# Attention and two MLPs on one core: the keys' products of a pair of heads as 24 matmuls of 64 rows and 128 columns in place of 12 of 128 rows and 256 columns

## The chip, the core and the metric

The kernel runs on one core of a Trainium2 chip. A core has TensorE (PE, with its weight loads PEld), VectorE (DVE), ScalarE (ACT), GpSimd (POOL), SyncE (SP) and 16 DMA engines. The metric is the device time of one execution in microseconds. The kernel before took 882.99 us, the median of three runs (882.97 to 883.67).

## The reference

Three stages follow each other: an attention with exponential features for 4 batches of 8 heads, and two MLPs over the 2304 rows that it gives.

```
def phi(x):                                   # x: 576 x 64 per head
    proj = x @ w_phi                          # w_phi: 64 x 128
    proj = proj - max(abs(proj), axis=-1)
    return concat([exp(proj), exp(-proj)])    # 576 x 256
q_p, k_p = phi(q), phi(k)
kv  = k_p.T @ v ;  z = sum(k_p, over the tokens)
out = (q_p @ kv) / (q_p @ z + 1e-06)
x = out.transpose(0, 2, 1, 3).reshape(2304, 512)
x = leaky(x @ w_in) @ w_out                   # leaky(h) = max(0.01 h, h), 512 -> 2048 -> 512
x = mish(x @ w_in2) @ w_out2                  # 512 -> 2048 -> 512
```

The change touches `k @ w_phi` and the subtraction of the largest absolute value behind it, for the first 512 of the 576 tokens.

## The kernel before

**Pairs and rounds.** The 32 heads are worked on as 16 pairs. `attention(n)` is one round, in which different pairs stand at different steps: pair n+2 is loaded and transposed, pair n+1 is multiplied by `w_phi` (`q_proj` for the queries, `k_proj` for the keys), pair n has its exponentials taken and its `kv` summed, pair n-1 is multiplied out (`nd`), and pair n-2 is normalised and turned back. Between them the weights of the first MLP are prepared (`extra`). The instructions of each engine run in the order in which this code writes them; PE, ACT and DVE each go through their own list and wait for each other by semaphores. Behind the attention come the two MLPs, some 740 of the 881 us.

**The keys' product.** A pair's keys lie transposed in `kth` and `ktl`, a high part rounded to fp32r and the remainder: 128 rows (two tokens of neighbouring places, 64 values each) by 512 columns (4 column groups of 128 for the two heads). `w_phi` lies in `wbh` and `wbl`, high and low part, as a block diagonal of 128 rows and 256 columns: the upper 64 rows meet the first 128 columns, the lower 64 rows the second, zeros elsewhere. One matmul takes a column group as its weights and streams the 256 columns of `wbh` or `wbl`; three such products (high by high, high by low, low by high) add up. A round has 12 of them: 6 into a PSUM tile `xt` (its pool has one buffer) and then 6 into a bank of the ring `a` (`bank("a")`, four banks in turn). The source line of all is L441.

**The guard.** `k_guard` takes each bank's maximum of the absolute values over 128 features (L429) and subtracts it (L430), on DVE. The result is `kd`, whose exponentials ACT takes a round later (L454).

**The queries' product** just ahead of it (`q_proj`, L469) is made of matmuls that use 64 rows of the array each, the upper and the lower half in turn, into four banks of the ring `a`; ACT copies these to `qd` (L471), and POOL takes the maximum over the partitions. The ring goes on: the keys' bank `a` is the one that held the first of the queries' four products.

**Behind the keys' block** stand on PE the products of the leftover tokens (L95 to L97, every other round), the transposes of the next pair (L402), the turning back (L561, into `xt` too), L535 and L512.

Of the kernel before, what the change touches and what calls it, by code (L numbers as in the profile page):

```python
# [9 lines left out]
F32 = mybir.dt.float32  # L10
# [10 lines left out]
def attention_two_mlps_kernel(  # L21
# [12 lines left out]
    nc = tc.nc  # L34
    B, H, S, D = q.shape
    NT, DM = out.shape
    DFF = w1_in.shape[1]
    F = w_phi.shape[1]
    P = 128
# [3 lines left out]
    NM = MAIN // P  # L43
# [26 lines left out]
    pa = tc.alloc_tile_pool(name="pa", bufs=1, space=PSUM)  # L70
    dr = tc.alloc_tile_pool(name="dr", bufs=1, space=bass.MemoryType.DRAM)
    ap = tc.alloc_tile_pool(name="ap", bufs=2, reuse_waits="tile")
# [3 lines left out]
    xt = {}  # L76
# [10 lines left out]
    def bank(ring):  # L87
        return rings[ring].tile([P, 512], F32, tag=ring, name=ring)
# [5 lines left out]
    def three(o, wh_, wl_, xh, xl, start=True, stop=True, **kw):  # L94
        nc.tensor.matmul(out=o, lhsT=wh_, rhs=xh, start=start, stop=False, **kw)  # L95
        nc.tensor.matmul(out=o, lhsT=wh_, rhs=xl, start=False, stop=False, **kw)  # L96
        nc.tensor.matmul(out=o, lhsT=wl_, rhs=xh, start=False, stop=stop, **kw)  # L97
# [40 lines left out]
    class Loads:  # L138
# [5 lines left out]
        def load(self):  # L144
            while not self.held and (self.rest or self.at < len(self.units) and places.open(places.stages)):
                self.half()
# [163 lines left out]
    with tc.manual_schedule():  # L310
# [28 lines left out]
        st = [dict() for _ in range(PAIRS)]  # L339
# [29 lines left out]
        def values(i):  # L369
            b, p = divmod(i, NP)  # L370
            h0 = 2 * p
            vm = st[i]["vm"] = vmain[i % NV]
            for h in range(2):
                nc.sync.dma_start(out=vm[:, h, :, 0:D], in_=v[b, h0 + h, 0:MAIN, :].rearrange("(p t) d -> p t d", t=NM))
            vl = st[i]["vl"] = vleft[i % NV]
            for r in range(2):
                nc.sync.dma_start(out=vl[r * LEFT:(r + 1) * LEFT, r, 0:D], in_=v[b, h0 + r, MAIN:S, :])
# [10 lines left out]
        wbh = ap.tile([P, 2 * F], F32R, name="wbh", bufs=1)  # L388
        wbl = ap.tile([P, 2 * F], F32R, name="wbl", bufs=1)
# [37 lines left out]
        def k_guard(src, n, kd):  # L427
            mx = ap.tile([P, n], F32, tag=f"mx{n}", name="mx")
            nc.vector.tensor_reduce(out=mx, in_=src, axis=AX.X, op=ALU.max, apply_absolute_value=True)  # L429
            nc.vector.tensor_tensor(  # L430
                out=kd, in0=src, in1=mx.unsqueeze(2).to_broadcast([P, n, F]), op=ALU.subtract)

        def k_proj(i, c, own=True):
            s = st[i]
            if c == 0:
                s["kd"] = ap.tile([P, 2, NM, F], F32, tag="kd", name="kd")
            t = pa.tile([P, 512], F32, tag="xt", name="xt") if c == 0 and own else bank("a")
            for n, (x, w) in enumerate((("kh", wbh), ("kh", wbl), ("kl", wbh))):
                for j in range(2):
                    u = slice((2 * c + j) * P, (2 * c + j + 1) * P)  # L440
                    nc.tensor.matmul(out=t[:, j * 2 * F:(j + 1) * 2 * F], lhsT=s[x][:, u], rhs=w,  # L441
                                     start=(n == 0 and j == 0), stop=(n == 2), skip_group_check=True)
            return lambda: k_guard(t.rearrange("p (n f) -> p n f", f=F), NM, s["kd"][:, c])

        def k_proj_left(i):
            l = lf[i // 2]
            l["kd"] = ap.tile([P, 2, F], F32, tag="kdl", name="kdl", bufs=1)
            t = bank("a")
            three(t[:, 0:2 * F], l["h"][:, 0:P], l["l"][:, 0:P], wbh, wbl)
            k_guard(t[:, 0:2 * F].rearrange("p (n f) -> p n f", f=F), 2, l["kd"])  # L450
# [6 lines left out]
        def q_proj(i, h):  # L457
            s = st[i]
            if "qd" not in s:
                s["qd"] = ap.tile([P, 2, S], F32, tag="qd", name="qd")  # L460
                s["qm"] = ap.tile([P, 2, S], F32, tag="qm", name="qm", bufs=1)
            todo = []
            for o in range(2):
                n = HM + (h == o) * LEFT
                todo.append((o, bank("a"), n, h * (HM + (1 - o) * LEFT), (1 - o) * (HM + h * LEFT)))
            for x, (w, q_) in enumerate(((wbh, "qh"), (wbh, "ql"), (wbl, "qh"))):
                for o, t, n, c0, d0 in todo:
                    r = slice(o * D, (o + 1) * D)
                    nc.tensor.matmul(out=t[:, 0:n], lhsT=w[r, o * F:(o + 1) * F], rhs=s[q_][r, c0:c0 + n], start=(x == 0), stop=(x == 2))  # L469
            for o, t, n, c0, d0 in todo:  # L470
                nc.scalar.activation(out=s["qd"][:, h, d0:d0 + n], in_=t[:, 0:n], func=AF.Copy)  # L471
            qd, qm = s["qd"][:, h, :], s["qm"][:, h, :]
            nc.gpsimd.partition_all_reduce(qm, qd, P, bass_isa.ReduceOp.absmax)  # L473
# [44 lines left out]
        def kv_copy(i):  # L518
            s = st[i]
            s["kv"] = ap.tile([P, 4, D + 1], F32, tag="kv", name="kv", bufs=1)  # L520
            nc.scalar.activation(out=s["kv"], in_=s["kvp"][:, 0:4 * (D + 1)].rearrange("p (c n) -> p c n", n=D + 1), func=AF.Copy)
# [48 lines left out]
        def left_exp(i, a):  # L570
            if i % 2 == 0:
                lf[i // 2].setdefault("lp", []).append(exp(lf[i // 2]["kd"], "lp", 1 - 2 * a))

        def q_exp_first(h):
            if "qp" not in st[0]:
                st[0]["qp"] = [ap.tile([P, 2, S], F32, tag=f"qp{sg}", name="qp", bufs=1) for sg in (1, -1)]
            for x in range(2):
                nc.scalar.activation(out=st[0]["qp"][x][:, h], in_=st[0]["qm"][h], func=AF.Exp, scale=float(1 - 2 * x))

        def q_exp(i):  # L580
            st[i]["qp"] = [exp(st[i]["qd"], "qp", sg) for sg in (1, -1)]

        def k_exp(i, a):
            st[i].setdefault("kp", []).append(exp(st[i]["kd"], "kp", 1 - 2 * a))
# [19 lines left out]
        def attention(n):  # L604

            x, o, w, p, t = (i if 0 <= i < PAIRS else None for i in range(n - 2, n + 3))
            x_copy = lambda: None
            if n + 3 < PAIRS:  # L610
                load(n + 3)
            loads.half()
            if t is not None and t > 1:
                values(t)
            loads.half()
            if n > 0:
                if p is not None:
                    q_proj(p, 0)
                    q_proj(p, 1)
                kv_copy(o)  # L620
            if n == 1:
                q_exp_first(1)
            if x is not None and n < PAIRS:
                normalise(x)
            if p is not None:
                k_proj(p, 0, t is not None)()
                k_proj(p, 1)()
                if p % 2 == 0:
                    k_proj_left(p)
            if w is not None:  # L630
                for a in range(2):
                    if n > 0:
                        left_exp(w, a)
                    k_exp(w, a)
                    if n == 0:
                        q_proj(p, a)
            if n == 0:
                for a in range(2):
                    left_exp(0, a)
            extra(n, 0)  # L640
            if n == PAIRS - 1:
                fill(0)
            if n == 0:
                transposes(t, "q", "l")
                q_left(t)
                q_guard_first(0)
                transposes(t, "k")
                q_guard_first(1)
                q_exp_first(0)
            elif t is not None:  # L650
                transposes(t)
                q_left(t)
            if x is not None:
                x_copy = x_t(x)
            x_copy()
            extra(n, 1)
            if o is not None:
                nd(o)
            if p is not None:
                q_guard(p)  # L660
            extra(n, 2)
            if w is not None:
                if n > 0:
                    q_exp(w)
                for a in range(2):
                    kv(w, a)
            if p is None:
                normalise(o)
            if n == PAIRS - 1:
                fill(1)  # L670
# [427 lines left out]
        while todo:  # L1098
            u = todo.pop(0)
# [45 lines left out]
        while todo:  # L1145
            u = todo.pop(0)
# [569 lines left out]
        for x in (10, 11):  # L1716
            t = place("s%d" % x, F32, 2, DM, pool=late[0], name="more")
# [27 lines left out]
        for x in range(2):  # L1745
            t = place("st%d" % x, F32, 2, DM, pool=gp, name="more")
# [15 lines left out]
        for s in range(2 * 4 * OPS):  # L1762
            sb, n, fp = steps3[s]
# [60 lines left out]
```

## Time and profile before

| what | value |
|---|---|
| median of three runs | 882.99 us |
| profiled execution | 883.12 us |
| its span, first to last instruction | 881.3 us |
| PE busy | 874.3 us (99%) |
| DVE busy | 633.3 us (72%) |
| ACT busy | 502.6 us (57%) |
| mean granted TensorE clock | 0.999 |

PE is busy nearly all the time. Busy time of PE overlaps in the records (a matmul is 280 to 390 ns long there, while the next starts 110 to 220 ns later), so the distance from one start to the next is what a matmul costs; durations only show when it was held up. The profile's page gives sums over the whole execution, and the attention is its first 141 us; the timelines below are from there.

### The profile page before, as it was taken

The numbers are of one execution on the slowest core, as the hardware profiler recorded it, in microseconds if no ns is written. First come the engines' busy times: TensorE is split into PE (matmuls) and PEld (weight loads), VectorE is DVE, ScalarE is ACT, GpSimd is POOL, SyncE is SP. The second block draws the span as 40 slices with busy tenths as digits, with TensorE's granted clock in tenths as the row PEclk, the third lists the DMA queues.
The fourth block names the chain that finished last, engine by engine and source line by source line (L and its number), as shares of the span: only waits on it lengthen the run. The fifth ranks groups of instructions, "written<-read, shape, count | busy, mean of one in ns | idle before, by whom it ended". The sixth has DMA issues, their size and how long they took to land.

```text
span 881.3 us, 17024 instructions
## 1 busy us (share of the span) xinstructions
PE 874.3 (99%) x6497; PEld 754.1 (86%) x6497; DVE 633.3 (72%) x1056; ACT 502.6 (57%) x828; POOL 78.5 (9%) x62
## 2 busy tenths in 40 slices
PE   9999999999999999999999999999999999999997
PEld 7999999888888888888988888888888888888887
DVE  8999998688988626889886328676655488655575
ACT  6899998656565545544454326444444477444442
POOL 4646452000000000000000000000000000000000
PEclk9999999999999999999999999999999999999999
DMA  6653430179788867899962454888875899876662
GB/s 176 173 144 99 110 103 3 61 251 324 265 291 275 287 229 251 253 375 362 348 202 85 136 177 171 292 313 274 304 258 188 283 371 397 235 226 221 201 179 60
DMA packets 145585, 197.28 MB, mean 224 GB/s; under 512 B 50912, under 2 KB 82272, under 8 KB 145504
## 3 DMA queue, kind: packets, MB, share of 16 engines
q1 hardware_dynamic: 116096, 143.36, 50.6%
q10 hardware_dynamic: 29408, 52.84, 17.1%
q8 instruction: 51, 0.84, 0.4%
q14 instruction: 30, 0.25, 0.1%
HBM read 119.60 MB, written 76.55 MB: 223 GB/s over the span
## 4 chain that ended last, share of the span: by engine, by line
PE 96%; ACT 2%; DMA 0%; DVE 0%; issue 0%; SPq 0%; ACTq 0%
PE b L95 14%; PE b L97 14%; PE b L96 14%; PE a L95 13%; PE a L96 13%; PE a L97 13%; PE outs L535 3%; PE kvp L512 3%; PE a L469 1%; PE a L402 1%; PE a L441 1%; PE xt L441 1%; PE xt L561 1%; PE kvp L515 1%; ACT qp L454 0%; ACT kp L454 0%
## 5 line engine op out<-in xcount | busy, mean ns | idle before, releaser
L92 DVE TENSOR_TENSOR g<-raw,g 128x1024 fp32r<-128x1024 f32 (+1 forms) x64 | 77.1, 1205 | 54.4 <-ACT g L91 54.3
L91 ACT ACTIVATE g<-raw 128x1024 fp32r<-128x1024 f32 (+1 forms) x64 | 66.9, 1046 | 66.5 <-PE b L97 37.0
L92 DVE TENSOR_TENSOR gl<-raw,gh 128x512 fp32r<-128x512 f32 x72 | 49.7, 690 | 60.0 <-ACT gh L91 57.7
L91 ACT ACTIVATE gh<-raw 128x512 fp32r<-128x512 f32 x72 | 45.2, 628 | 60.8 <-PE b L97 24.6
L473 POOL PARTITION_ALL_REDUCE qm<-qd x30 | 64.2, 2189 | 45.1 <-ACT qd L471 42.1
L96 PE MATMUL b<-gl,wo 128*128 128x512 f32 (+1 forms) x192 | 67.9, 354 | 0.0
L95 PE MATMUL b<-gh,wo 128*128 128x512 f32 (+1 forms) x192 | 67.9, 354 | 0.0
L97 PE MATMUL b<-gh,wo 128*128 128x512 f32 (+1 forms) x192 | 67.9, 354 | 0.0
L95 PE MATMUL b<-win,w 128*128 128x512 f32 x128 | 49.9, 390 | 0.0
L96 PE MATMUL b<-win,w 128*128 128x512 f32 x128 | 49.9, 390 | 0.0
L95 PE MATMUL a<-gh,wo 128*128 128x512 f32 x128 | 49.8, 389 | 0.0
L96 PE MATMUL a<-gl,wo 128*128 128x512 f32 x128 | 49.8, 389 | 0.0
L97 PE MATMUL a<-gh,wo 128*128 128x512 f32 x128 | 49.8, 389 | 0.0
L97 PE MATMUL b<-win,w 128*128 128x512 f32 x128 | 49.8, 389 | 0.0
L95 PE MATMUL b<-g,wo 128*128 128x512 f32 x128 | 49.8, 389 | 0.0
L96 PE MATMUL b<-g,wo 128*128 128x512 f32 x128 | 49.8, 389 | 0.0
L97 PE MATMUL b<-g,wo 128*128 128x512 f32 x128 | 49.8, 389 | 0.0
L917 DVE TENSOR_TENSOR g<-b,z 128x512 f32<-128x512 f32 x31 | 21.4, 689 | 36.2 <-PE b L97 33.4
L96 PEld LDWEIGHTS b<-gl,wo 128*128 128x128 f32 x192 | 36.3, 189 | 5.0
L97 PEld LDWEIGHTS b<-gh,wo 128*128 128x128 f32 x192 | 36.3, 189 | 5.0
L95 PEld LDWEIGHTS b<-gh,wo 128*128 128x128 f32 x192 | 36.3, 189 | 4.9
L1514 DVE TENSOR_TENSOR g<-g,g 128x512 f32<-128x512 f32 x32 | 22.1, 689 | 23.0 <-ACT g L1498 16.5
(325 smaller groups left out, 2535.5 us busy)
## 6 DMA issues: line engine op xcount, KB each, us to landing
raw<-gp SPq DMA_DIRECT2D x56, 512.0 KB, 5.4
raw<-gd ACTq DMA_DIRECT2D x72, 256.0 KB, 3.8
gd<-g ACTq DMA_DIRECT2D x70, 256.0 KB, 3.9
stage<-in_moe_w_out_dram SPq DMA_DIRECT2D x32, 512.0 KB, 5.6
gp<-g SPq DMA_DIRECT2D x64, 256.0 KB, 2.8
stage<-in_moe_w_in_dram SPq DMA_DIRECT2D x26, 512.0 KB, 6.0
gp<-g ACTq DMA_DIRECT2D x48, 256.0 KB, 3.1
scr<-more SPq DMA_DIRECT2D x24, 256.0 KB, 5.1
```

The source lines that it names most:

```text
L91: nc.scalar.activation(out=hi, in_=src, func=AF.Copy)
L92: nc.vector.tensor_tensor(out=lo, in0=src, in1=hi.bitcast(F32), op=ALU.subtract)
L95: nc.tensor.matmul(out=o, lhsT=wh_, rhs=xh, start=start, stop=False, **kw)
L96: nc.tensor.matmul(out=o, lhsT=wh_, rhs=xl, start=False, stop=False, **kw)
L97: nc.tensor.matmul(out=o, lhsT=wl_, rhs=xh, start=False, stop=stop, **kw)
L402: nc.tensor.transpose(out=t[:, j * P:(j + 1) * P], in_=s[nm + "n"].rearrange("p h t d -> p (h t d)")[:, j * P:(j + 1) * P], identity=ident)
L441: nc.tensor.matmul(out=t[:, j * 2 * F:(j + 1) * 2 * F], lhsT=s[x][:, u], rhs=w, start=(n == 0 and j == 0), stop=(n == 2), skip_group_check ...
L473: nc.gpsimd.partition_all_reduce(qm, qd, P, bass_isa.ReduceOp.absmax)
L512: nc.tensor.matmul(out=both[r, h, a, :], lhsT=s["kp"][a][:, h, t, r], rhs=s["vm"][:, h, t, :], start=(a == 0 and h == 0 and t == 0), stop= ...
L535: nc.tensor.matmul(out=g[u // 2][r, u % 2, h], lhsT=s["qp"][a][:, h, q0 + r.start:q0 + r.stop], rhs=s["kv"][:, 2 * h + a], start=(a == 0), ...
L917: nc.vector.tensor_tensor(out=c, in0=x["Y"], in1=cur[0].z7[n % 2], op=ALU.add)
L1514: nc.vector.tensor_tensor(out=out_, in0=in0, in1=in1, op=ALU.subtract)
```

## The change

A new function, `k_proj_rows`, takes the place of the two calls of `k_proj` in each round (15 rounds; the first pair's keys are still multiplied by `k_proj`). Each matmul takes 64 rows of the keys, the upper half (tokens of even parity) or the lower one (odd parity), and the 128 columns of `w_phi` that aren't zeros for these rows. Upper and lower halves alternate. The even tokens' products go to the `xt` bank, the odd ones' to the bank of the ring `a`, so each bank now holds both heads' tokens of one parity. The guards run behind all 24 and write `kd` with a stride.

```
+        def k_proj_rows(i, own):
+            s = st[i]
+            s["kd"] = ap.tile([P, 2, NM, F], F32, tag="kd", name="kd")
+            ts = [pa.tile([P, 512], F32, tag="xt", name="xt") if own else bank("a"), bank("a")]
+            for x, w in (("kh", wbh), ("kh", wbl), ("kl", wbh)):
+                for u in range(NM):
+                    for r in range(2):
+                        rows = slice(r * D, (r + 1) * D)
+                        nc.tensor.matmul(out=ts[r][:, u * F:(u + 1) * F], lhsT=s[x][rows, u * P:(u + 1) * P], rhs=w[rows, r * F:(r + 1) * F],
+                                         start=(x == "kh" and w is wbh and u == 0), stop=(x == "kl"), skip_group_check=True)
+            for r, t in enumerate(ts):
+                k_guard(t.rearrange("p (n f) -> p n f", f=F), NM, s["kd"].rearrange("p h (j r) f -> p r (h j) f", r=2)[:, r])
...
             if p is not None:
-                k_proj(p, 0, t is not None)()
-                k_proj(p, 1)()
+                k_proj_rows(p, t is not None)
                 if p % 2 == 0:
                     k_proj_left(p)
```

On PE, the keys' block of the third round stands like this before; `xt` and `a` are the two banks, `kth` and `ktl` the keys' parts, and what an instruction waits for stands in brackets:

```order
L469 MATMUL a<-qth,wbl 128x320
L441 MATMUL xt<-wbh,kth 128x256 [waits Activation_49]
L441 MATMUL xt<-wbh,kth 128x256
L441 MATMUL xt<-wbl,kth 128x256 x2
L441 MATMUL xt<-wbh,ktl 128x256 x2
L441 MATMUL a<-wbh,kth 128x256 [waits Activation_49]
L441 MATMUL a<-wbh,kth 128x256
L441 MATMUL a<-wbl,kth 128x256 x2
L441 MATMUL a<-wbh,ktl 128x256 x2
L402 MATMUL a<-ident,qn 128x128 [waits DMAHW3_49,Activation_49]
```

And the same place with the change, its first eight and last two rows:

```order
L482 MATMUL a<-qth,wbl 128x320
L453 MATMUL xt<-wbh,kth 128x128 [waits Activation_49]
L453 MATMUL a<-wbh,kth 128x128 [waits Activation_49]
L453 MATMUL xt<-wbh,kth 128x128
L453 MATMUL a<-wbh,kth 128x128
L453 MATMUL xt<-wbh,kth 128x128
L453 MATMUL a<-wbh,kth 128x128
L453 MATMUL xt<-wbh,kth 128x128
...
L453 MATMUL a<-wbh,ktl 128x128
L402 MATMUL a<-ident,qn 128x128 [waits DMAHW3_49,Activation_49]
```

The first instruction into the bank `a`, which waits for ACT, has moved from the seventh place of the block to the second. On DVE the guards keep their places; in the round after that they read, with the change (before, the subtractions have 128x512 as their shape):

```order
L564 TENSOR_TENSOR xn<-outs,den 128x640 [waits DVE_49]
L429 TENSOR_REDUCE mx<-xt 128x4 [waits PE_49]
L430 TENSOR_TENSOR kd<-xt,mx 128x4x128 [waits DVE_49]
L429 TENSOR_REDUCE mx<-a 128x4 [waits PE_49]
L430 TENSOR_TENSOR kd<-a,mx 128x4x128 [waits DVE_49]
```

What moved is not on DVE's own list: its first guard waits for the last matmul into `xt`, which now stands last but one in the block.

## Rows read from the trace of the kernel before

**Rows 1.** The page: busy us (share of the span) and instructions of each engine.

```profile
PE 874.3 (99%) x6497; PEld 754.1 (86%) x6497; DVE 633.3 (72%) x1056; ACT 502.6 (57%) x828; POOL 78.5 (9%) x62
```

**Rows 2.** Attention: stretch, length, busy PE, PEld, DVE, ACT, POOL (instructions), clock, DMA.

```profile
0.00:141.00 141.00, 138.67 (x2626) 129.84 (x2628) 130.02 (x241) 124.62 (x233) 77.39 (x62) 1.00 0.47 126
```

**Rows 3.** Timeline of PE, one round: start, us, line, operation, shape, count.

```profile
61.12 1.10 PE L512 MATMUL kvp<-vmain,kp 128*64 128x65 f32 x32
62.05 0.39 PE L515 MATMUL kvp<-vleft,lp 128*64 128x130 f32 x4
...
64.29 0.31 PE L469 MATMUL a<-qth,wbl 64*128 64x320 f32 x2
64.52 0.51 PE L441 MATMUL xt<-wbh,kth 128*128 128x256 f32 x2
64.86 0.40 PE L441 MATMUL xt<-wbl,kth 128*128 128x256 f32 x2
65.10 0.40 PE L441 MATMUL xt<-wbh,ktl 128*128 128x256 f32 x2
65.34 0.40 PE L441 MATMUL a<-wbh,kth 128*128 128x256 f32 x2
...
66.06 0.60 PE L402 MATMUL a<-ident,qn 128*128 128x128 f32 x4
```

**Rows 4.** Timeline of the weight loads, the queries' block of that round.

```profile
63.53 0.19 PEld L469 LDWEIGHTS a<-qth,wbh 64*128 64x128 f32 x2 [0.18 <-issue]
63.64 0.19 PEld L469 LDWEIGHTS a<-qtl,wbh 64*128 64x128 f32 x2
```

**Rows 5.** L564 at 67.5: timeline of both, then duration in ns, min/median/max.

```profile
67.47 0.30 PEld L564 LDWEIGHTS kvp<-eyes,xn 128*128 128x128 f32 x2
...
67.58 0.33 PE L564 MATMUL kvp<-eyes,xn 128*128 128x64 f32 x2
...
L564 PE MATMUL kvp<-eyes,xn x2: 222/248/275, 67.6 to 67.6; 128*128 128x64 f32 x2
```

**Rows 6.** Timelines of ACT and PE: first copies and keys' blocks of three rounds.

```profile
20.21 0.44 ACT L471 ACTIVATE qd<-a 128x320 f32<-128x320 f32 x1
20.14 0.39 PE L441 MATMUL xt<-wbh,kth 128*128 128x256 f32 x1
...
74.29 0.44 ACT L471 ACTIVATE qd<-a 128x320 f32<-128x320 f32 x1
73.72 0.50 PE L441 MATMUL xt<-wbh,kth 128*128 128x256 f32 x2
74.78 0.50 PE L441 MATMUL a<-wbh,kth 128*128 128x256 f32 x2
75.60 0.28 PE L95 MATMUL a<-wbh,lh 128*128 128x256 f32 x1
...
128.06 0.44 ACT L471 ACTIVATE qd<-a 128x320 f32<-128x320 f32 x1
128.09 0.39 PE L441 MATMUL xt<-wbh,kth 128*128 128x256 f32 x1
```

**Rows 7.** Who waited for L441 (us, times); then DVE's guard at 65.5.

```profile
  DVE mx L429: 4.2, 8
...
65.54 0.69 DVE L429 TENSOR_REDUCE mx<-xt 128x4 f32<-128x512 f32 x1
```

**Rows 8.** Timelines of DVE, ACT and PE, 43 to 47 us.

```profile
44.00 0.68 DVE L92 TENSOR_TENSOR qtl<-a,qth 128x512 fp32r<-128x512 f32 x1
43.77 0.63 ACT L210 ACTIVATE c<-c 128x512 f32<-128x512 f32 x1 [1.48 <-DVE c L200]
44.31 2.21 ACT L454 ACTIVATE qp<-qd 128x1152 f32<-128x1152 f32 x2
46.55 1.32 ACT L471 ACTIVATE qd<-a 128x320 f32<-128x320 f32 x4
46.45 0.39 PE L441 MATMUL xt<-wbh,kth 128*128 128x256 f32 x1
```

## The prediction

> **What bounds the kernel now.** I began with the page: PE is busy for 874.3 of 881.3 us [rows 1], so what lengthens PE's own sequence in the attention stage lengthens the kernel unless a later wait absorbs it. The table by stretches says the same of the first 141 us, where the attention runs: PE 138.67, DVE 130.02 and ACT 124.62 us busy, at the full granted clock [rows 2]. So PE leads there, but DVE and ACT have only a tenth to spare: whoever is made to start later will soon be late.
>
> The timeline of PE then shows one round of the attention [rows 3], some 9 us from 63.5 on: queries' products (L469), keys' products (L441), transposes (L402). The keys' block takes from 64.52 to 66.06, 1.54 us, for 12 matmuls of 256 columns: two in 0.24 us (64.86, 65.10, 65.34), 0.118 to 0.12 each. Two places are slower. The pair at 64.52 takes 0.34 us, and the block starts 0.23 us after the last rows of L469: PE has gone from 64 rows to 128, and the first load cannot hide behind the matmul before. That change of shape costs about 0.1 us at each of the two.
>
> **The loads decide the array's time.** The queries' block is already made of 64-row products in the two halves of the rows. Its weight loads [rows 4] come in twos at 63.53 and 63.64: both halves load at once (two loads end within the 0.19 us of one), and each half can load again only 0.11 us later, although a load has 64 rows. The same step stands at L564, where the two loads of 128 columns take 0.30 us together where one shows 0.19, so the second starts 0.11 after the first, and the two matmuls of only 64 columns end 0.11 us apart: 67.58 + 0.22, and 67.58 + 0.33 [rows 5] (0.22 is the shorter of the two). A load of 128 columns is thus worth 0.11 us however short the matmul behind it.
>
> So the edit brings, for each of 15 pairs of heads, 24 loads in place of 12, and 128 columns behind each in place of 256. Each half gets 12 of them, one per 0.111 us by rows 5; before, 12 matmuls took 0.12 each. The streaming is halved, and the loads are not. In array time alone the block stays at about 12 x 0.11. The bounds of this unseen form: 0.064 us per matmul and half from below (256 columns at 2.4 GHz, the clock's upper level, which rows 2 show granted, stream 0.107; half of that, and the 0.011 that the 0.118 per matmul holds beyond it), 0.23 from above (rival B). I take 0.111, the nearest row: same load, same rows of the array in rows 4.
>
> **The wait that the change moves forward.** Block and ACT are tied by a bank. The ring "a" has four banks; the keys' matmuls into "a" use the bank that held the first queries' product, which ACT must have copied out (L471). Before, those matmuls are the second half of the block, 0.8 us after its start, by which time the copy is mostly done. Now the second instruction of the block writes "a", and PE issues in order, so the xt matmuls behind it wait too. In the round of 73.72 the copy ends at 74.73, 1.01 us after the block's start and later than even the old place, and the "a" matmul starts 0.05 us behind it, at 74.78 [rows 6]. I measured the same distance in all 13 middle rounds (the first: copy 20.21 + 0.44, block 20.14, so 0.51; the last 0.41): it lies between 0.24 and 1.01 and sums to 6.07 us. The floor of 0.24 is where ACT has nothing else to do and waits for the product itself.
>
> **The sum.** The new block, from its old start: the copy's end, 0.05 to the "a" matmul, 11 steps of 0.111 = 1.22, then the change to 128 rows, which now stands behind the block: 0.23 less the 0.06 that a 128-column matmul streams less = 0.17, and about 0.08 for the first load of the next shape (0.1 before an L95, half of it before a transpose). That is 1.52 us behind the copy's end. Over 13 rounds: 6.07 + 13 x 1.52 = 25.8 us. Before: eleven blocks of 1.52 to 1.54 and two that already waited, 1.89 (73.72 to 75.60) and 1.85, together 20.6 us. Difference +5.2 us. The block of 11.1 us stands outside, since no queries' product goes ahead of it there: 0. The last one (137.5) has both its banks from "a", their copies done by 0.22 us: +0.2.
>
> **What goes late next.** DVE's guard (maximum and subtraction, L429 and L430) takes xt first. It began 1.02 us after the block's start (65.54), when six matmuls were done; in the interleaved order xt is complete only after eleven of twelve steps, at least 0.24 + 0.05 + 1.11 + 0.32 (last xt matmul's start to the guard, as before: 65.22, the second of the two at 65.10, to 65.54) = 1.72. DVE already waited there 8 times, 4.2 us in all [rows 7]; now it waits in each round and ends some 0.7 us later, while PE is later by 0.25 to 0.5. In most rounds that is hidden: the split for the next queries ends at least 0.8 us before they start (at 44.68 against 46.45 - 0.99 = 45.46 [rows 8]). It is not hidden where ACT has to wait for DVE. DVE makes c (L200); ACT, idle for 1.48 us until then, takes it at 43.77, then two exponentials of 2.21 us together, then the copies at 46.55. With DVE 1.4 us late there (two rounds' delay) and PE 1.0, that copy ends 0.4 us further behind its block, 0.99 in place of 0.54. Following the rounds of 46, 64 and 101 us so, and letting the next rounds win back what ACT gains on a later PE (the 1.01 of 73.72 becomes about 0.7), I come to +1 us more. Sum: 5.2 + 0.2 + 1.0 = +6.4. The guard's subtractions write kd by tokens of one parity, still 512 elements each: 0, with 0.69 us for the maximum over as many elements in rows 7, and at most a tenth of that as a price. PE stays the bound behind 141 us, so the delay goes through to the end.
>
> The profiled execution took 883.1 us in all (span 881.3), 0.1 above the median of 883.0. So 883.1 + 6.4 = 889.5, or 889.4 against the median, which I forecast. Own range: loads at 0.107 and no knock-on +4.5, loads at 0.118 and twice the knock-on +8.4; with half a us or more for the changes of shape, 886.5 to 893.
>
> **Rival A, not slower: the halves run at the pace of the streaming.** If a half's load hid behind the other half's matmul, a step would be 0.064 us. For it: the two halves of rows 4 do load together. Against it: each half's own loads are still 0.11 apart there. Block: copy's end + 0.05 + 0.70 + 0.25 = 1.00; 6.07 + 13.0 = 19.1, 1.5 us below before: 881.6, with some knock-on 882 to 884. It decides below 0.074 us a step, where the sum equals before. To be faster by over 0.2% the copies would have to come earlier too, and nothing moves ACT ahead. The Trainium skill's page TensorEngine Tiling (Array Packing), section Theoretical Speedup, gives up to 2x where the contracted side is at most 64; that is this rival, and the loads in rows 4 and 5 speak against its full size here. Chance 0.12.
>
> **Rival B: narrow products run at the rate of plain f32.** No fp32r matmul in the trace has fewer than 256 columns, so a slower mode for 128 isn't excluded. The f32 products of L512 [rows 3] show the rate: 32 records, two for each of 16 matmuls, 8 in each column half, from 61.12 to 62.05, 0.117 for 65 columns, 1.8 ns a column where fp32r has 0.47. At 128 columns that is 0.23 a step: 6.07 + 13 x (0.05 + 2.53 + 0.25) = 42.9, +22.3 us, and 1.6 for the last: some 906. These rows tell nothing of fp32r itself, so it stays open. Chance 0.11.
>
> **Rival C: load and matmul in a half follow each other.** 0.107 + 0.053 + 0.011 = 0.17 a step: 6.07 + 13 x 2.17 = 34.3, +13.7, with the last block 897 to 898. Against: in rows 3 two loads and two matmuls of 256 columns go through in 0.24 us, so the one runs beside the other. Chance 0.07.
>
> **Chances and range.** Forecast 0.70, A 0.12, B 0.11, C 0.07. What differs by less than 0.2% (1.8 us) can't be told from no change. A is split 0.08 within and 0.04 faster; all else is slower: 0.88. The range 883.5 to 900 holds the forecast, C, and about half of A; B and the rest of A, 0.17, lie outside.
>
> **What would show it.** Right: the 24 matmuls in twos, 0.11 us apart; a gap of 0.3 us or more between the first xt and the first "a" matmul, released by ACT's L484 (the old L471); a DVE wait on xt in nearly all rounds, well over 4.2 us in sum; blocks of 1.75 to 2.6 us; the end of the attention some 6 us later, and everything behind it of the same length. Wrong: steps of 0.06 or of 0.17 and more, the "a" matmul right behind the first xt, or a stage behind 141 us that gives the delay back.

## The result and the profile after

The changed kernel takes 892.98 us (median of four runs, 892.67 to 893.23) against 883.06: ratio 1.0111, 95% interval 1.0095 to 1.0127. It is slower by 9.9 us; the forecast was 6.4. The page of after gives the span and the engines' busy time (as in [rows 1]):

```profile
span 891.4 us, 17384 instructions
PE 878.8 (99%) x6677; PEld 755.0 (85%) x6677; DVE 630.4 (71%) x1056; ACT 502.9 (56%) x828; POOL 75.3 (8%) x62
```

PE's busy time grew by 4.5 us, the span by 10.1: PE does a little more and waits more. One ordinary round on PE's timeline after (start, length, line, count; this answers to [rows 3] and [rows 6]):

```profile
77.29 0.41 PE L482 MATMUL a<-qth,wbh 64*128 64x320 f32 x2
...
78.05 0.31 PE L482 MATMUL a<-qth,wbl 64*128 64x320 f32 x2
78.19 0.22 PE L453 MATMUL xt<-wbh,kth 64*128 64x128 f32 x1
78.58 0.32 PE L453 MATMUL a<-wbh,kth 64*128 64x128 f32 x1 [0.17 <-ACT qd L484]
78.58 0.32 PE L453 MATMUL xt<-wbh,kth 64*128 64x128 f32 x1
78.74 0.27 PE L453 MATMUL a<-wbh,kth 64*128 64x128 f32 x1
...
79.86 0.27 PE L453 MATMUL a<-wbh,ktl 64*128 64x128 f32 x1
80.06 0.39 PE L95 MATMUL a<-wbh,lh 128*128 128x256 f32 x1
...
81.63 0.63 PE L574 MATMUL xt<-ident,xn 128*128 128x128 f32 x4
```

Three things can be read there. The first xt matmul follows the queries at 78.19 without the old gap; the second of the block waits until 78.58 for ACT's copy, which runs at 78.09 in this row of ACT's timeline:

```profile
78.09 0.44 ACT L484 ACTIVATE qd<-a 128x320 f32<-128x320 f32 x1
```

From 78.58 to 79.86 the twelve steps go by in twos. And between the block's end (80.06) and the turning back into xt (81.63) lie 1.57 us, with 1.34 us of work in them. DVE's timeline shows what happens meanwhile (answers to [rows 7]):

```profile
80.06 0.69 DVE L429 TENSOR_REDUCE mx<-xt 128x4 f32<-128x512 f32 x1 [1.49 <-PE xt L453]
80.79 0.69 DVE L430 TENSOR_TENSOR kd<-xt,mx 128x512 f32<-128x512 f32 x1
```

DVE had waited 1.49 us for xt, and reads the bank until 81.48; L574 writes it 0.15 later. Before, DVE was done with the bank at 66.96 and PE came to it later by its own work alone, at 67.15 (rows of DVE's and PE's timelines before):

```profile
66.27 0.69 DVE L430 TENSOR_TENSOR kd<-xt,mx 128x512 f32<-128x512 f32 x1
67.15 0.60 PE L561 MATMUL xt<-ident,xn 128*128 128x128 f32 x4
```

The waits of the attention after, PE's (us, times, longest), and who waited for L453:

```profile
PE a L453 <- ACT qd L484: 3.9, 14, 0.7
PE xt L574 <- DVE kd L430: 1.5, 6, 0.3
...
  DVE mx L429: 17.0, 14
```

DVE's 4.2 us of waiting became 17.0. The waits of PE are understated in such a table, because the tail of the matmul before counts as busy; distances between starts are whole. Over the 12 rounds from the third on, whose sum went from 108.69 to 117.05 us, the distances are these (each summed from the starts of the first matmul of a part in each round):

| part of a round, 12 rounds | before | after | difference |
|---|---|---|---|
| first queries' matmul to first keys' matmul | 11.90 | 10.77 | -1.13 |
| keys' block, to what follows | 19.08 | 23.65 | +4.57 |
| from there to the turning back (L561, L574) | 14.15 | 18.80 | +4.65 |
| from there to the next queries | 63.56 | 63.85 | +0.28 |
| sum | 108.69 | 117.05 | +8.37 |

The other 1.7 us of the span: 0.8 in the first and last rounds, and 0.9 behind the attention, of which 0.5 stands at one place where the weights' way through DRAM (c from scr) is late and PE idles at 605.29:

```profile
605.29 0.50 PE L95 MATMUL b<-win,w 128*128 128x512 f32 x1 [0.35 <-ACT b L875]
```

No run followed that place up, so it is only read from the trace.

### The profile page after: what moved, and what is told of

It is laid out like the page before. It is cut to its first block, busy times and chain, and to the rows that moved or that the text cites. A ratio compares the mean times of both kernels' runs of the same rounds, so it can differ in the third digit from the quotient of the medians.

```text
span 891.4 us, 17384 instructions
## 1 busy us (share of the span) xinstructions
PE 878.8 (99%) x6677; PEld 755.0 (85%) x6677; DVE 630.4 (71%) x1056; ACT 502.9 (56%) x828; POOL 75.3 (8%) x62
## 3 DMA queue, kind: packets, MB, share of 16 engines
q10 hardware_dynamic: 29408, 52.84, 17.1%
## 4 chain that ended last, share of the span: by engine, by line
PE 93%; DVE 3%; ACT 2%; DMA 1%; issue 1%; SPq 0%; ACTq 0%; DVEq 0%
PE b L95 14%; PE b L96 14%; PE b L97 14%; PE a L95 13%; PE a L96 13%; PE a L97 13%; PE outs L548 3%; PE kvp L525 3%; PE a L453 2%; DVE mx L429 1%; PE a L482 1%; DVE kd L430 1%; PE xt L574 1%; PE a L402 1%; ACT qd L484 1%; DMA c<-scr 1%
## 5 line engine op out<-in xcount | busy, mean ns | idle before, releaser
L95 PE MATMUL b<-gh,wo 128*128 128x512 f32 (+1 forms) x192 | 67.9, 354 | 0.0
L95 PE MATMUL b<-win,w 128*128 128x512 f32 x128 | 50.0, 391 | 0.3 <-ACT b L875 0.3
L95 PE MATMUL a<-gh,wo 128*128 128x512 f32 x128 | 49.8, 389 | 0.0
L95 PE MATMUL b<-g,wo 128*128 128x512 f32 x128 | 49.8, 389 | 0.0
L95 PEld LDWEIGHTS b<-gh,wo 128*128 128x128 f32 x192 | 36.3, 189 | 5.0
```

## The experiments

Theory: the narrow products are no faster, because a load of 128 columns costs 0.11 us; what costs is the order, by two waits: "a" ahead of ACT's copy, and the turning back behind DVE's guard, since xt is complete only at the block's end. Rivals: the narrow or the half-row products themselves cost; or DVE or ACT set the round, and PE only shows it.

**Wide products in the changed order.**

```
...
for n_, (x, w) in enumerate((("kh", wbh), ("kh", wbl), ("kl", wbh))):
    for j in range(2):
        for c in range(2):                                   # banks xt and a in turn
            u = slice((2 * c + j) * P, (2 * c + j + 1) * P)  # 128 rows, 256 columns as before
            nc.tensor.matmul(out=ts[c][...], lhsT=s[x][:, u], rhs=w, ...)
...
```

> The 12 products of 128 rows and 256 columns of before, but in the changed order: a matmul into xt and one into a in turn, the guards behind all twelve. Theory (the order costs, not the narrow form): the second matmul waits for ACT's first copy, and xt is complete only at the block's end, so the turning back (x_t) waits for DVE's guard as it does with the change; with 0.118 us a step the block is some 0.08 us shorter or longer than with the change, so 891 to 895 us. Rival (the 64-row products, their loads or the changes of shape cost): near before, 883 to 885 us.

892.17 us, 1.0102 (1.0085 to 1.0119) of before: as slow as the change. Order alone gives nearly all of it; the halves and the narrow products are worth nothing that these runs tell apart. Over the same 12 rounds, queries and keys' block together grew by 2.7 us here (3.4 with the change) and the way to the turning back by 5.6 (4.65). PE's waits in this kernel:

```profile
PE xt L574 <- DVE kd L430: 3.8, 12, 0.4
PE a L453 <- ACT qd L484: 1.3, 5, 0.4
```

**All 128 rows in each of the 24.**

```
-  lhsT=s[x][rows, u * P:(u + 1) * P], rhs=w[rows, r * F:(r + 1) * F],
+  lhsT=s[x][:, u * P:(u + 1) * P], rhs=w[:, r * F:(r + 1) * F],
```

> The changed kernel with all 128 rows of the keys in each of the 24 matmuls (the other half meets zeros), still 128 columns: the halves of the array no longer work side by side. Theory (a load of 128 columns costs 0.11 us, however little streams behind it, and two halves load at once): 24 steps of 0.11 in a row, plus 1.3 us a round, 15 rounds: 910 to 914 us. Rival (the streaming of the columns sets the step): 24 steps of 0.064, plus 0.2 us a round: 894 to 897 us.

909.89 us in the one run, hardly below what was expected. On PE's timeline the 24 now go one by one, 0.11 us apart, though only 128 columns stream:

```profile
64.66 0.27 PE L452 MATMUL a<-wbh,kth 128*128 128x128 f32 x1
64.77 0.28 PE L452 MATMUL xt<-wbh,kth 128*128 128x128 f32 x1
64.88 0.28 PE L452 MATMUL a<-wbh,kth 128*128 128x128 f32 x1
65.00 0.28 PE L452 MATMUL xt<-wbh,kth 128*128 128x128 f32 x1
```

So the two halves do work side by side in the change; that saves what the doubled number of loads costs, and no more.

**Half the columns, and half the load.** Two kernels, with the full width in the first pass only:

```
...                                              # the first kernel
+  c_ = F if x == "kh" and w is wbh else D      # half the columns streamed
   out=ts[r][:, u * F:u * F + c_], lhsT=s[x][rows, u * P:(u + 1) * P], rhs=w[rows, r * F:r * F + c_]
...                                              # the second kernel
+  c_ = P if x == "kh" and w is wbh else D      # half the tokens loaded
   out=ts[r][0:c_, u * F:(u + 1) * F], lhsT=s[x][rows, u * P:u * P + c_], rhs=w[rows, r * F:(r + 1) * F]
```

> The changed kernel with only 64 of the 128 columns streamed in the second and third of the three passes (16 of the 24 matmuls); the corrections of half the features are left out, the weight loads are the same. Theory (the load sets the step): steps of 0.11 us in those passes too, 891 to 894 us. Rival (the streaming of 128 columns sets it, by a slower mode of narrow products): steps of 0.055 to 0.06, some 6 us less, 885 to 888.

> The changed kernel with weight loads of only 64 of the 128 tokens in the second and third pass; the corrections of half the tokens are left out, 128 columns are streamed as with the change. Theory (the load sets the step): steps of about 0.06 us in those passes, 0.4 us less a round, of which the change to a 64-column shape inside the block takes back up to 0.2: 886 to 891 us. Rival (streaming or the product itself sets it): steps stay at 0.11, 891 to 895.

891.97 and 887.72 us, one run each. With half the columns the steps stay (the last rows of PE's timeline of one block):

```profile
59.34 0.27 PE L454 MATMUL a<-wbl,kth 64*128 64x64 f32 x1
59.34 0.27 PE L454 MATMUL xt<-wbl,kth 64*128 64x64 f32 x1
59.45 0.27 PE L454 MATMUL a<-wbl,kth 64*128 64x64 f32 x1
```

With half the load they fall to 0.06 as soon as the narrow loads begin, all 128 columns streaming:

```profile
57.27 0.27 PE L454 MATMUL a<-wbh,kth 64*128 64x128 f32 x1
57.38 0.27 PE L454 MATMUL a<-wbh,kth 64*128 64x128 f32 x1
...
57.50 0.22 PE L454 MATMUL a<-wbl,kth 64*64 64x128 f32 x1
57.55 0.22 PE L454 MATMUL a<-wbl,kth 64*64 64x128 f32 x1
57.61 0.22 PE L454 MATMUL a<-wbl,kth 64*64 64x128 f32 x1
```

So the load sets the step. Rival B of the prediction, a slower mode for narrow products, is out: 128 columns pass in 0.06 us.

**The guards in the other order: a dose of the second wait.**

```
-  for r, t in enumerate(ts):
+  for r, t in reversed(list(enumerate(ts))):
       k_guard(...)
```

> The changed kernel with the two guards in the other order on DVE: bank a first, xt second. A dose of the second wait. Theory (x_t on PE waits until DVE has read xt): it now waits for two guards, 2.74 us, in place of one, 1.42: the time from the block's end to x_t goes from 1.57 to about 2.9 us, plus 1.3 us in 13 rounds: 907 to 911 us. Rival (x_t's wait is not on the guard, or PE's time is set elsewhere): 892 to 895.

911.06 us (median of 908.27 to 912.21), 1.031 (1.0291 to 1.0329). The distance from the block to the turning back went from 1.57 to 2.99 us in each of the 12 rounds that have one behind a block in xt, and PE's wait from 1.5 to 17.5 us:

```profile
PE xt L574 <- DVE kd L430: 17.5, 11, 1.7
```

1.42 us in 12 rounds is 17.1 (the expectation counted 13 rounds). The sum of these rounds rose by 16.4, from 117.05 to 133.47 us: ACT's copy was no longer late in any of them, which gave back 1.1, and 0.4 came elsewhere. What DVE needs for xt is on the path, at nearly full price.

The median's 18.1 us above the change hold something else besides. In the profiled execution (span 908.7 us against 891.4) the granted clock is 0.50, the lower level of 1.2 GHz, from 21.7 to 24.4 us, after 3.7 us in which PE had been busy for 2.9. This falls into the second round, which has no turning back: from the end of its block to the next queries it took 7.54 us, with the change 5.99. The one of the four executions with a mean clock of 1.0 took 908.27 us, 15.3 above the change.

**ACT's first two copies swapped: meant as a dose of the first wait.**

```
-  for o, t, n, c0, d0 in todo:
+  for o, t, n, c0, d0 in todo if h else todo[::-1]:
       nc.scalar.activation(out=s["qd"][:, h, d0:d0 + n], ...)
```

> The changed kernel with ACT's first two copies of the queries' products in the other order, so the bank that the keys' products want comes free one copy (0.27 us) later. A dose of the first wait. Theory (the second matmul of the block waits for that copy): the gap ahead of the first a matmul grows from 0.39 to 0.66 us in each of 13 rounds: plus 3.5 us, 895.5 to 898 us. Rival (PE waits for something that ends later anyway, so that this gap is only time given back elsewhere): 892 to 894.

892.39 us, 1.0105 (1.0088 to 1.0122); missed, and the reason is in the trace: the "a" matmul waits for whichever copy comes first, now the shorter one, and starts 0.34 us after the first xt in place of 0.39:

```profile
77.52 0.22 PE L453 MATMUL xt<-wbh,kth 64*128 64x128 f32 x1
77.86 0.32 PE L453 MATMUL a<-wbh,kth 64*128 64x128 f32 x1
```

So the bank that it waits for is not the one named ahead of the prediction, that of the first product; that banks are handed on in the order of their release would explain it, but no run shows that. The dose was thus -0.045 us; an ordinary round became as much shorter (9.63 to 9.58 us from queries to queries), but the sum, 0.6 us, is too small for these runs to show.

**Work put between queries and keys: the first wait taken away.**

```
   if p is not None:
       q_proj(p, 0)
       q_proj(p, 1)
+  if o < PAIRS - 1:
+      kv(o, 1)            # from the end of the round before; values(t) is loaded behind it
   kv_copy(o)
...
-      for a in range(2):
-          kv(w, a)
+      kv(w, 0)
+      if w == PAIRS - 1:
+          kv(w, 1)
```

> The changed kernel with one move: the second half of a pair's kv sum (1.15 us of PE's work that needs no bank of the ring a) goes from the end of a round to the place between the queries' and the keys' products. Theory: the first matmul into a finds its bank copied out by ACT; the gap of 0.39 to 0.93 us between the first xt and the first a matmul goes, its floor of 0.28 and the lumps: minus 4 to 6 us, 887 to 889 us; x_t still waits for the guard. Rival (ACT or DVE set the round's length, and PE only waits in another place): 891 to 893.

894.3 us, 1.0127 (1.0112 to 1.0142): missed. In most rounds the wait did go, and the block fell from 1.87 to 1.49 us. But products of 64 columns between two runs of 64 rows cost two more changes of the array's shape, 0.25 us, and the wait for the guard grew by 0.1. What was left, 0.04 a round, was outweighed by rounds in which, for the most part, the queries' block came out longer: the sum of the 12 rounds is 118.24 us, 1.2 above the change. PE's timeline shows the two gaps, 0.23 at 77.53 to 77.76 and 0.2 behind the last matmul before 79.07:

```profile
77.53 0.31 PE L482 MATMUL a<-qth,wbl 64*128 64x320 f32 x2
77.76 1.16 PE L525 MATMUL kvp<-vmain,kp 128*64 128x65 f32 x32
78.75 0.39 PE L528 MATMUL kvp<-vleft,lp 128*64 128x130 f32 x4
...
79.07 0.32 PE L453 MATMUL xt<-wbh,kth 64*128 64x128 f32 x1
79.12 0.33 PE L453 MATMUL a<-wbh,kth 64*128 64x128 f32 x1
```

**nd ahead of the turning back: meant to hide the second wait.**

```
+  if o is not None:
+      nd(o)
   if x is not None:
       x_copy = x_t(x)
   x_copy()
   extra(n, 1)
-  if o is not None:
-      nd(o)
```

> The changed kernel with one swap: the product with the queries (nd) goes ahead of the turning back (x_t), so 2.3 us of PE's work that does not touch the bank xt stand between the keys' block and x_t. Theory: x_t waited 0.33 to 0.47 us per round for DVE's guard on xt, 12 rounds; that goes, minus 4 to 5 us: 888 to 889 us. Rival (DVE's late start holds up the round by another way, the queries' split or ACT's copies): the wait comes back elsewhere and the time stays at 892 to 893.

903.36 us, 1.0226 (1.021 to 1.0241): missed by far. ACT copies xt and xc out in its written order, ahead of the round's exponentials, and now gets them 2 us later. ACT's largest wait there, and PE's behind it:

```profile
ACT xc L578 <- PE kvp L577: 19.6, 13, 2.1
...
PE a L453 <- ACT qd L484: 5.3, 14, 0.9
PE kvp L525 <- ACT xc L578: 4.1, 13, 0.3
```

A new wait took the place of the old one, so this run tells nothing for or against the guard's.

**The upper half some steps ahead: the second wait taken away by order alone.**

```
+  steps = [(x, w, u) for x, w in (("kh", wbh), ("kh", wbl), ("kl", wbh)) for u in range(NM)]
+  ahead = 4 if own else 0                       # and 6
+  for m in range(len(steps) + ahead):
+      for r, at in ((0, m), (1, m - ahead)):
+          if 0 <= at < len(steps):
+              x, w, u = steps[at]               # then the matmul as in the change, into ts[r]
```

> The changed kernel with the upper half (xt) four steps ahead of the lower half (a): four xt products alone, eight in twos, four a products alone. Theory: the four steps of 0.11 us cover the copy's wait (0.39), so the block is about as long as with the change, 16 steps; xt is complete 0.44 us ahead of the block's end, so x_t no longer waits for the guard and its distance from the block falls from 1.57 to 1.15 or 1.25: minus 4 to 5 us, 888 to 889 us. Rival (DVE or ACT would hold the round in another place): 892 to 893.

> The same with six steps ahead, 18 in all. Theory: x_t's wait is gone already with four, so two more steps only lengthen the block by 0.22 us, in the rounds where the copy is done by then, and save the rest of the wait where ACT is late: 889.5 to 892 us. Rival (the earlier start of DVE's guard, not x_t's wait, is what helps): as low as with four or lower, 886 to 888.

889.15 us (1.0073, 1.0058 to 1.0088) and 889.29 (1.0074, 1.0058 to 1.0091). With four, 3.8 us are won back, and PE's waits have no line for xt behind DVE any more; the way from the block to the turning back sums to 14.94 us in the 12 rounds (18.80 with the change, 14.15 before). The block is as long as with the change, 1.87 us; the turning back comes 1.33 us behind it in this round and 1.15 in those without leftover products, in place of 1.57, and DVE starts ahead of the block's end:

```profile
58.31 0.60 PE L456 MATMUL a<-wbh,ktl 64*128 64x128 f32 x4
58.85 0.38 PE L95 MATMUL a<-wbh,lh 128*128 128x256 f32 x1
...
60.18 0.60 PE L577 MATMUL xt<-ident,xn 128*128 128x128 f32 x4
```

```profile
58.46 0.69 DVE L429 TENSOR_REDUCE mx<-xt 128x4 f32<-128x512 f32 x1 [1.13 <-PE xt L456]
```

With six the time is no different, a little below what was expected; the reason is told at the end, under what was unexpected. None of these versions beats the kernel before.

## Why the prediction was right, and which step failed

**Array time: right.** The steps were 0.11 us, as taken from L564 and the queries' loads, with half the columns as well; rivals A, B and C fell. Behind the copy's end the block took 1.54 us in each of the 13 rounds, whether the copy was late (2.41 - 0.87 in the round of 68 us) or not (1.87 - 0.34). Of the 1.52 summed, 1.44 were for this; the other 0.08, the first load of the next shape, falls behind the block. It measured 0.06 ahead of a transpose and 0.1 ahead of an L95: with four steps ahead, where PE no longer waits for the guard, the way to the turning back is 1.15 and 1.33 us, before it was 1.09 and 1.23.

**The first wait: right in place, too dear in size.** The "a" matmul waits for ACT in each round, and starts 0.39 us or more behind the first xt. The distances from the block's old start to the copy's end, taken as 6.07, became some 4.4: each delay of PE lets ACT catch up, and in nine of the 13 rounds the copy now comes at its floor. That ACT wins time on a later PE stood in the text, but only as a discount on the knock-on. The blocks, counted from the queries on, grew by 3.8 us in the 13 rounds (3.44 in the twelve of the table, 0.34 in the second round); with some 1.0 for the first loads behind them this is 4.8, where 5.2 was summed. So the sum came near because a copy taken 1.7 us too dear and steps taken 1.3 us too cheap nearly cancel.

**What goes late next: this step failed.** It was to be hidden "in most rounds", with 1.0 us from ACT's chain. DVE's later start and its longer waits came as forecast (14 waits, 17.0 us). The step asked who needs DVE's next results, the queries' split, and found slack. It did not ask who needs the bank that the guard reads: the turning back, 1.1 to 1.2 us behind the block on PE, writes into xt. The guard ends 1.42 us behind the block's end, so PE waits in each round, some 0.2 us where leftover products stand between and 0.4 where not. Of the 4.65 us that this way grew by in twelve rounds, some 3.7 are this wait, and the rest the first loads named above. The swapped guards made the wait 17.1 us longer and the twelve rounds 16.4, and four steps ahead took it away (-3.8). The knock-on through ACT did not come: four or five of the 13 rounds have a late copy, where eight or nine had one before, and the copy of the round of 46 us, forecast to end 0.99 us behind its block's old start in place of 0.54, ended 0.60 behind it.

**The rest.** That the delay goes through to the end held; 0.9 us more came behind the attention, half of it at a late transfer. Two sums of the working come out otherwise and change nothing: the own range's low end is +4.8 and not +4.5 (5.4 less 0.004 for each of 11 steps in 13 rounds), and rival B's time is 906.9 and not some 906.

So 6.4 was 5.2 + 0.2 + 1.0, and the span's 10.1 is about 4.8 + 0.2 + 3.7 + 0.3 for the rest of the rounds, 0.2 in the first rounds and 0.9 behind the attention. The direction and the first wait were understood. That 892.98 still lies within the own range, at its very end of 893, is partly luck: a wait of 3.7 us was missing, and it stood against a knock-on of 1.0 that did not come and 0.4 too much in the first sum.

## What to carry to other kernels

Where each matmul brings its own weights, count the loads before the columns: two narrow products in two halves of the rows cost two loads side by side, the same time as one wide product whose stream just covers its load (0.11 us against 0.118 here). When two banks are filled in turn in place of one after the other, both are wanted at the start and both are free only at the end; look for who empties the one and for who next writes the other, on the critical engine above all. And read a wait's price by making it longer as well as by taking it away: the three ways here of taking a wait away by moving other work, or a copy, all brought something else with them.

## What the hardware showed unexpectedly

**Matmuls in the two halves of the rows don't start in written order.** With six steps ahead, seven xt products are written ahead of the first a product. PE's timeline has only four of them ahead:

```profile
57.07 0.56 PE L456 MATMUL xt<-wbh,kth 64*128 64x128 f32 x4
57.46 0.33 PE L456 MATMUL a<-wbh,kth 64*128 64x128 f32 x1
57.47 0.39 PE L456 MATMUL xt<-wbl,kth 64*128 64x128 f32 x2
```

Once the copy was done, the a product started ahead of three xt products written before it, which follow 0.11 us apart, the step of the loads. So the lead shrank to four by itself, and the block stayed at 1.87 us. The changed kernel shows it too: in its second round the first xt product starts at 19.83, and a queries' product written before it at 19.88. What stands ahead of the prediction, that an engine's instructions run in the order in which the code writes them, thus does not hold for the starts of PE's matmuls in different halves of the rows. In an ordinary round of the change this doesn't help, since there the second matmul is the one that waits on ACT, and no xt product behind it starts before it does (78.58).

**A change of the array's shape has a price at each place.** The step from the queries' 64 rows to 128 rows cost some 0.1 us of gap (0.23 between the starts before, 0.12 with the change, where the shape stays) and 0.1 us in the first load; in the run with kv between the products, two more such steps cost 0.25 us a round together. From loads of 128 columns to loads of 64, both in 64 rows, nothing was lost (57.38 to 57.50).
